# Seven-product units of a fused attention and two-layer MoE kernel: sums in two PSUM tiles by turns, two products of the last unit swapped, no hand-over margin in the planner

## The chip, the cores and the metric

The kernel runs on one core of one Trainium2 chip. The metric is the device time of one execution in microseconds; the kernel before takes 1227.4 us, the median of three runs (1226.18 to 1228.07).

## The reference

An attention block with head mixing before and after the softmax feeds a two-matrix layer with a hard-swish gate, and that feeds a second layer of two up-projections, their product, and two further matrices. All arrays are float32 (B 4, H 12, S 448, D 64).

```python
scores = einsum('bhij,hg->bgij', scale * q @ k.T, w_pre)
attn = softmax(scores)                        # over the last axis
x = einsum('bhij,hg->bgij', attn, w_post) @ v  # then (1792, 768)
h = x @ w_in                                  # 768 -> 2048
g = h * clip(h + 3, 0, 6) / 6
x = g @ w_out                                 # 2048 -> 768
h = (x @ w1) * (x @ w2) @ w3                  # 768 -> 1024 -> 1024
return h @ w_out2                             # 1024 -> 768
```

## The kernel before, in words

Products are made with float32 values split into a high and a low part of a faster format: weight and activation both become a high half (a cast) and a low half (a subtraction), and each product of two values is three matmuls (high by high, high by low, low by high). The kernel multiplies the last two matrices w3 and w_out first (tile `w34`), so the second layer ends with one product by a 1024 x 768 matrix.

The work on the chip goes through these stages: attention, slot by slot (tiles `sc`, `pre`, `post`, `val`); the up-projection by w_in (`up`, for batches 0 and 3 directly, for batches 1 and 2 in seven-product units); the down-projection by w_out (`dn`); `w34`; the second layer's two up-projections in 16 seven-product units (`step`, 8 for each pair of batches, weights in tile `block`); and the final product in 6 seven-product units (3 for each pair of batches, weights in tile `wb`, activations split into `gh` and, in space of the earlier `act` tiles, under that name).

A seven-product unit computes a two by two block product with seven products in place of eight: the function `seven` (L812). Its operands are sums and differences made beforehand on VectorE (`combine` L1096, `rows2` L1257 and the joined weights). Its products are called p1 to p7 in the code, each of K x 3 matmuls of 128 x 448: nine in the units of the `up` and `step` stages (K = 3), twelve in the final stage (K = 4). They add up in three PSUM sums: cs takes p1, p6, p7 and p4 in this order, bs takes p5 and p3, as_ takes p2. In between ScalarE copies the running sum out: k1 after p1, k5 after p5, k6 after p6 (`keep`, the copies of L831). VectorE adds: c11 = as_ + k1 after p2, c12 = bs + k6 after p3, c22 = cs + k5 after p7 (`plus`, L834). p4 adds to cs and must wait for c22; what remains in cs is c21. In the kernel before, cs and bs are the two halves of one PSUM tile `pair`, and as_ is a half of a second tile, `other`, which the unit takes with p2. All PSUM tiles have one shape, [128, 2, 512] float32, and there are four of them. The next unit's p1 may follow as soon as p7 is done.

The order of instructions on every engine is fixed when the program is built, by a planner (`Plan`). Each operation has an engine or a choice of engines, an estimated duration, a priority (a due time) and its predecessors. `Plan.run` (L118) simulates the engines: whenever one is free it takes the waiting operation with the smallest due time that is ready and for whose new buffers there is room. An operation gets ready when its last predecessor has ended plus a hand-over (`HOP`, by the predecessor's engine); if it is for TensorE the hand-over has, unless the predecessor is also on TensorE, a margin of `SLACK` = 400 ns on top. The instructions are then written in the order found, and the engines run them in that order. The semaphores between engines are placed by the language's tile framework from the tiles that instructions read and write.

Due times come from sums of the values in `URGE`: the stage of the up units begins at M1, that of the down products at N1 = M1 + 8 F, `w34` at W0 = N1 + 4 D1, the `step` units at M2 = W0 + W, the final units at N2 = M2 + 16 U2, and offsets such as `gsum` (loads and splits of the final stage's activations), `joined`, `w2` and `wd` (weights) move single kinds of work against these.

Of the kernel before, what the change touches and what calls it, by code (L numbers as in the profile page):

```python
# [20 lines left out]
B, H, S, D = 4, 12, 448, 64  # L21
# [28 lines left out]
def query_order():  # L50
# [9 lines left out]

URGE = dict(pPool=13.287, pACT=19737.186, pDVE=67509.792, pOut=0.285, pGuard=376.043, pCopy=21.334, pRest=107.553, pEvac=52.694, load0=33.466, load=-4.77, gather=-168.494, pre=-140.104, max=-8.516, exp=27.495, norm=15.87, post=2.04, evac=43.38, values=32.185, step=8.267, vload=-54.801, vload0=-30.207, lead=-15.369, begin=-9.6, consts=-75.04, moe=75.017, rows=-53.563, win=-71.545, wout=-22.784, w34=60.311, w2=140.007, unit0=3.845, unit1=6.452, down1=165.725, unit2=13.355, down2=98.964, wo=-88.875, wd=-84.964, narrow=-53.097, sums=98.427, w34us=69.836, pHalf=621.884, halve=10.141, gsum=-54.585, joined=-78.357, pairs=-27.451, lag=-51.378, mix=75.595, wo1=23.777)


SHARED = dict(
# [2 lines left out]
    wo=tuple(f"z{i}" for i in range(9)) + ("w0", "w1", "w2") + tuple(f"y{i}" for i in range(28)),  # L69
# [20 lines left out]
class Plan:  # L90
# [1 line left out]

    HOP = dict(Host=0, PE=200, ACT=150, DVE=130, Pool=130, SP=0)
    DMA_START, DMA_END, FREED = 1100, 910, 180
    SLACK = 400

    def __init__(self, room):
        self.room, self.ops, self.chains = dict(room), [], {}
# [33 lines left out]
    def run(self):  # L132
# [18 lines left out]
        while events:  # L151
            now, done = heapq.heappop(events)
            if done >= 0:
                op = self.ops[done]
                for tag, n in op["gives"].items():
                    self.room[tag] += n
                for x in op["holds"]:
                    x.held -= 1
                    if not x.held:
                        freed.append((now + self.FREED, x.tag))  # L160
                        heapq.heappush(events, (now + self.FREED, -1))
                for n in followers[done]:
                    hop = self.HOP[op["eng"]]
                    if "PE" in n["choice"]:
                        hop = dict(DVE=240 + self.SLACK, ACT=hop + self.SLACK, Pool=hop + self.SLACK, PE=0).get(op["eng"], hop)
                    n["ready"] = max(n["ready"], now + hop)
                    n["left"] -= 1
                    if not n["left"]:
                        for e in n["choice"]:
                            heapq.heappush(waiting[e], (n["prio"], n["id"]))  # L170
                        heapq.heappush(events, (n["ready"], -1))
            if events and events[0][0] <= now:
                continue
            while freed and freed[0][0] <= now:
                tag = freed.popleft()[1]
                for t in PARTS.get(tag, (tag,)):
                    self.room[t] += 1
            for e, heap in waiting.items():
                if free[e] > now:
                    continue  # L180
                skipped = []
                while heap:
                    prio, i = heapq.heappop(heap)
                    op = self.ops[i]
                    if op["eng"]:
                        continue
                    first = next(iter(op["choice"]))
                    homes = None
                    if op["ready"] <= now and (e == first or free[first] > now + URGE["p" + op["wait"]]) and (port <= now or e not in op["port"]) and (not op["apart"] or burst <= now):
                        if op["chain"] is None or self.chains[op["chain"]][0] == i:  # L190
                            homes = self.places(op["new"])
                    if homes is None:
                        skipped.append((prio, i))
                        continue
                    for x, tag in zip(op["new"], homes):
                        x.tag = tag
                        for t in PARTS.get(tag, (tag,)):
                            self.room[t] -= 1
                    if op["chain"] is not None:
                        self.chains[op["chain"]].popleft()  # L200
                        heapq.heappush(events, (now, -1))
                    op["eng"] = e
                    if e == "SP":
                        free[e] = now + op["issue"]
                        wire = max(now + self.DMA_START, wire) + op["choice"][e]
                        end = wire + self.DMA_END
                    else:
                        free[e] = end = now + op["choice"][e]
                        if e in op["port"]:
                            port = end  # L210
                        if op["apart"]:
                            burst = now + op["apart"]
                            heapq.heappush(events, (burst, -1))
                    heapq.heappush(events, (free[e], -1))
                    heapq.heappush(events, (end, i))
                    op["start"] = now
                    order.append(op)
                    break
                for x in skipped:
                    heapq.heappush(heap, x)  # L220
# [10 lines left out]
def attention_moe(ctx: ExitStack, tc, qd, kd, vd, consts, w_in, w_out, w1, w2, w3t, w4, out):  # L231
    nc = tc.nc
# [69 lines left out]
    plan = Plan({**rooms, **{tag: 0 if tag in later else x[3] for tag, x in BUFS.items()}})  # L302
# [506 lines left out]
        def __call__(self):  # L809
            return self.part(self.of.t)  # L810

    def seven(prio, K, ws, xs, before, after=()):  # L812

        pair, other = Buf("up"), Buf("up")
        t, v = Buf("t"), Buf("v")
        cs, bs, as_ = (View(pair, lambda t: t[:, 0, :S]), View(pair, lambda t: t[:, 1, :S]), View(other, lambda t: t[:, 0, :S]))

        def times(n, at, o, start, new=(), after=()):
            (bufs, parts), (xh, xl) = ws[n], xs[n]

            def emit():
                take(*new)
                for c in range(K):
                    wh, wl = (part()[:, col(c)] for part in parts)
                    mm(o(), wh, xh.t[:, c], start and c == 0, False, skip_group_check=not start)
                    mm(o(), wh, xl.t[:, c], False, False, skip_group_check=not start)
                    mm(o(), wl, xh.t[:, c], False, c == K - 1, skip_group_check=not start)
            return plan.add("PE", 607 * K, prio(at), emit, read=(*bufs, xh, xl), new=new, hold=(o.of,), after=after)

        def keep(at, x, k, o, after):  # L830
            return plan.add("ACT", 530, prio(at), lambda: nc.scalar.copy(x.t[:, k], o()), after=after, hold=(pair, x))  # L831

        def plus(at, x, k, o, after):
            return plan.add("DVE", 620, prio(at), lambda: nc.vector.tensor_tensor(out=x.t[:, k], in0=o(), in1=x.t[:, k], op=ALU.add), after=after, hold=(o.of, x))  # L834

        p1 = times(0, 0, cs, True, (pair, t, v), (*before, *after))
        k1 = keep(0, t, 0, cs, (p1,))
        p5 = times(1, 1, bs, True, after=(p1,))
        k5 = keep(1, v, 0, bs, (p5,))
        p6 = times(2, 3, cs, False, after=(k1,))  # L840
        k6 = keep(3, t, 1, cs, (p6,))
        p2 = times(3, 4, as_, True, (other,))
        c11 = plus(4, t, 0, as_, (p2, k1))
        p3 = times(4, 5, bs, False, after=(k5,))
        c12 = plus(5, t, 1, bs, (p3, k6))
        p7 = times(5, 6, cs, False, after=(k6,))
        c22 = plus(6, v, 0, cs, (p7, k5))
        p4 = times(6, 9, cs, False, after=(c22,))
        return t, v, cs, p7, p4, (p2, p3), c11, c12, c22, keep

# [179 lines left out]
    joined = {}  # L1030
# [266 lines left out]
    for pr in range(2):  # L1297
        gs = rows2(pr)
        for m in range(3):
            at = N2 + D2 * (3 * pr + m)  # L1300
            prio = lambda n: at + n * D2 / 10
            t, v, cs, p7, p4, p3, c11, c12, c22, keep = seven(prio, 4, blocks2(at + URGE["wd"], m), gs, before)
            before = (p7,)
            c21 = keep(9, v, 1, cs, (p4,))
            for k, b in enumerate(ORDER[2 * pr:2 * pr + 2]):
                for q, x, y, done in ((0, t, k, (c11, c12)[k]), (1, v, 1 - k, (c21, c22)[k])):
                    plan.add("SP", 900, prio(9), lambda m=m, b=b, q=q, x=x, y=y: nc.sync.dma_start(
                        out=out[col(2 * m + q), b * S:(b + 1) * S], in_=x.t[:, y]), after=(done,), hold=(x,))
# [52 lines left out]
```

## Time and profile before

| | |
|---|---|
| median of three runs | 1227.4 us |
| the profiled execution | 1230.79 us, of which the span from first to last instruction is 1229.0 us |
| granted TensorE clock | 0.999 of full speed over the span |
| TensorE matmul busy | 1185.4 us (96%) |
| TensorE weight load busy | 973.5 us (79%) |
| VectorE, ScalarE, GpSimd busy | 830.4, 630.6, 194.4 us |
| DMA | 259.87 MB, queue of the sync engine 63.2% of 16 engines' span |

PE stands for TensorE's matmuls, PEld for its weight loads, which overlap them, DVE for VectorE, ACT for ScalarE, POOL for GpSimd, SP for the sync engine that issues the transfers. Instructions are grouped by the source line that wrote them, and many come from one helper: all matmuls have line 239, all low halves and differences line 242, casts and plain copies lines 344 (ACT) and 346 (DVE). So tiles tell them apart. "Idle before" is the time the engine had nothing running ahead of an instruction, and the arrow names the engine whose instruction ended that wait.

### The profile page before, as it was taken

To read this page: it belongs to the slowest core of one execution; us is meant where nothing else is said; L and a number is where in the kernel's file an instruction comes from. 1 tells how busy PE (TensorE), PEld (TensorE's weight loads), DVE (VectorE), ACT (ScalarE), POOL (GpSimd) and SP (SyncE) were. 2 spreads that over 40 slices of the span, in tenths; PEclk is the share of its full clock that TensorE was granted. 3 is DMA by queue.
4 is the path that set the end of the run, shared out by engine and by line. 5 is a ranking of instruction groups with operands and counts; after the bars stand their busy time and mean duration, and the time that the engine had idled before them with its cause. 6 is when DMAs were issued, how large, how long until landed. Compare 5 with 4: busy or idle time off the path is not lost. (4 is left out here: it accounts for less than half of the span.)

```text
span 1229.0 us, 29521 instructions
## 1 busy us (share of the span) xinstructions
PE 1185.4 (96%) x11904; PEld 973.5 (79%) x11904; DVE 830.4 (68%) x1364; ACT 630.6 (51%) x1203; POOL 194.4 (16%) x412
## 2 busy tenths in 40 slices
PE   8899999999989999999999999999999999998998
PEld 3556666666658888988999999998889998997887
DVE  3778687776688879743875647676854577478682
ACT  6657666566667566522664344443433354334351
POOL 2474565663231000000000000000000000000000
PEclk9999999999999999999999999999999999999999
DMA  6645653744844566732989798989864438387531
GB/s 217 180 152 198 198 196 133 228 163 157 278 130 156 178 212 218 252 135 76 328 298 326 250 290 307 338 303 346 288 217 149 126 109 305 112 293 244 180 124 68
DMA packets 132945, 259.87 MB, mean 211 GB/s; under 512 B 11880, under 2 KB 75208, under 8 KB 132808
## 3 DMA queue, kind: packets, MB, share of 16 engines
q1 hardware_dynamic: 132808, 257.98, 63.2%
q8 instruction: 94, 1.54, 0.5%
q14 instruction: 43, 0.35, 0.1%
HBM read 151.97 MB, written 67.26 MB: 178 GB/s over the span
## 5 line engine op out<-in xcount | busy, mean ns | idle before, releaser
L239 PE MATMUL up<-act,block 128*128 128x448 f32 x1008 | 208.5, 367 | 3.0 <-ACT t L831 2.4
L239 PEld LDWEIGHTS up<-act,block 128*128 128x128 f32 x1008 | 188.4, 188 | 22.7 <-ACT t L831 4.2
L239 PE MATMUL dn<-gs,act 128*128 128x448 f32 x720 | 151.3, 367 | 0.0
L239 PEld LDWEIGHTS post<-wt,e 60*64 60x64 f32 x5760 | 101.8, 135 | 55.5 <-issue 27.1
L239 PEld LDWEIGHTS dn<-gs,act 128*128 128x128 f32 x720 | 135.2, 188 | 12.2
L239 PE MATMUL up<-act,wide 128*128 128x448 f32 x630 | 135.4, 368 | 1.1 <-DVE v L834 0.3
L502 ACT ACTIVATE e<-pre,m 128x448 f32<-128x448 f32 (+1 forms) x184 | 116.3, 635 | 38.7 <-DVE m L496 18.7
L496 DVE TENSOR_REDUCE m<-pre 128x2 f32<-128x896 f32 (+1 forms) x92 | 99.8, 1085 | 43.1 <-PE pre L239 43.0
L239 PEld LDWEIGHTS up<-act,wide 128*128 128x128 f32 x630 | 117.4, 188 | 14.3 <-issue 1.3
L239 PE MATMUL post<-wt,e 60*64 60x60 f32 x5760 | 108.8, 220 | 10.9 <-issue 3.7
L710 ACT ACTIVATE raw<-raw 128x384 f32<-128x384 f32 (+1 forms) x140 | 72.0, 524 | 77.5 <-DMA raw<-w 38.0
L239 PE MATMUL pre<-g,wih 64*64 64x448 f32 x720 | 95.4, 565 | 6.0 <-issue 1.8
L239 PE MATMUL up<-act,wb 128*128 128x448 f32 x432 | 91.2, 367 | 7.7 <-ACT t L831 3.3
L834 DVE TENSOR_TENSOR t<-up,t 128x448 f32<-128x448 f32 x60 | 37.3, 622 | 90.0 <-PE up L239 85.4
L344 ACT CAST block<-raw 128x384 fp32r<-128x384 f32 x103 | 52.7, 515 | 87.6 <-PE up L239 75.4
L473 POOL MEMSET g<- 4x896 f32 x92 | 76.7, 835 | 117.2 <-PE pre L239 91.2
L239 PEld LDWEIGHTS up<-act,wb 128*128 128x128 f32 x432 | 80.4, 188 | 17.3 <-ACT t L831 5.2
L242 DVE TENSOR_TENSOR block<-raw,block 128x384 fp32r<-128x384 f32 x112 | 60.6, 553 | 28.0 <-ACT block L344 27.9
L718 ACT ACTIVATE raw<-raw 128x768 f32<-128x768 f32 (+1 forms) x70 | 55.7, 795 | 35.0 <-DVE raw L716 34.8
L239 PE MATMUL dn<-gs,wo 128*128 128x448 f32 x336 | 72.9, 368 | 0.0
L722 DVE SCALAR_TENSOR_TENSOR raw<-raw 128x384 int32<-128x384 int32 (+1 forms) x140 | 68.6, 525 | 1.2
L239 PEld LDWEIGHTS dn<-gs,wo 128*128 128x128 f32 x336 | 63.1, 188 | 5.9
(135 smaller groups left out, 1809.4 us busy)
## 6 DMA issues: line engine op xcount, KB each, us to landing
g<-s SPq DMA_DIRECT2D x180, 210.0 KB
raw<-w SPq DMA_DIRECT2D x48, 384.0 KB
graw<-g1dram SPq DMA_DIRECT2D x32, 448.0 KB
raw<-w_out SPq DMA_DIRECT2D x32, 384.0 KB
raw<-w_in SPq DMA_DIRECT2D x28, 384.0 KB
g1dram<-t SPq DMA_DIRECT2D x24, 448.0 KB
raw<-w3t SPq DMA_DIRECT2D x32, 256.0 KB
wraw<-w34dram SPq DMA_DIRECT2D x30, 256.0 KB
```

The lines of the kernel that those rows point to most:

```text
L239: nc.tensor.matmul(o, lhsT=lt, rhs=rh, start=start, stop=stop, **kw)
L242: eng.tensor_tensor(out=o, in0=a, in1=b, op=ALU.subtract)
L344: nc.scalar.copy(o, i)
L473: nc.gpsimd.memset(g.t[:BEFORE], 0.0)
L496: nc.vector.tensor_reduce(out=m.t[used], in_=pre.t[used, :, :S], axis=AX.X, op=ALU.max, negate=True)
L502: nc.scalar.activation(out=e.t[used, a_], in_=pre.t[used, a_, :S], func=ACTF.Exp, bias=m.t[used, a_:a_ + 1], accum_out=z.t[used, a_:a_ + 1])
L710: nc.scalar.mul(value()[:, halves[i]], f(bits(i))[:, :, 1], 2.0 ** -112)
L718: nc.scalar.activation(out=f(y), in_=f(y), func=ACTF.Prelu, alpha=-2.0 ** 32)
L722: two(out=m.t[:, halves[i]], in0=bits(i)[:, :, 0], scalar=29, in1=m.t[:, halves[i]], op0=ALU.logical_shift_right, op1=ALU.bitwise_or)
L834: return plan.add("DVE", 620, prio(at), lambda: nc.vector.tensor_tensor(out=x.t[:, k], in0=o(), in1=x.t[:, k], op=ALU.add), after=after, h ...
```

## The change

Three things. In `seven`, bs moves from the second half of `pair` to the first half of `other`, as_ to the second half of `other`; `other` is now taken with p5 instead of p2, and p2 comes after p5 (before, it had no predecessor in its unit). In the very last unit (`final`) p7 comes before p3, which waits for it. In the planner the margin `SLACK` is gone. Besides, 20 of the values in `URGE` are new.

```diff
-    SLACK = 400
...
-                        hop = dict(DVE=240 + self.SLACK, ACT=hop + self.SLACK, Pool=hop + self.SLACK, PE=0).get(op["eng"], hop)
+                        hop = dict(DVE=240, PE=0).get(op["eng"], hop)
...
-    def seven(prio, K, ws, xs, before, after=()):
+    def seven(prio, K, ws, xs, before, after=(), final=False):
...
-        cs, bs, as_ = (View(pair, lambda t: t[:, 0, :S]), View(pair, lambda t: t[:, 1, :S]), View(other, lambda t: t[:, 0, :S]))
+        cs, bs, as_ = (View(pair, lambda t: t[:, 0, :S]), View(other, lambda t: t[:, 0, :S]), View(other, lambda t: t[:, 1, :S]))
...
-            return plan.add("ACT", 530, prio(at), lambda: nc.scalar.copy(x.t[:, k], o()), after=after, hold=(pair, x))
+            return plan.add("ACT", 530, prio(at), lambda: nc.scalar.copy(x.t[:, k], o()), after=after, hold=(o.of, x))
...
-        p5 = times(1, 1, bs, True, after=(p1,))
+        p5 = times(1, 1, bs, True, (other,), (p1,))
...
-        p2 = times(3, 4, as_, True, (other,))
+        p2 = times(3, 4, as_, True, after=(p5,))
         c11 = plus(4, t, 0, as_, (p2, k1))
-        p3 = times(4, 5, bs, False, after=(k5,))
-        c12 = plus(5, t, 1, bs, (p3, k6))
-        p7 = times(5, 6, cs, False, after=(k6,))
-        c22 = plus(6, v, 0, cs, (p7, k5))
+        p7 = times(5, 5 if final else 6, cs, False, after=(k6,))
+        c22 = plus(5 if final else 6, v, 0, cs, (p7, k5))
+        p3 = times(4, 6 if final else 5, bs, False, after=(k5, p7) if final else (k5,))
+        c12 = plus(6 if final else 5, t, 1, bs, (p3, k6))
...
-            t, v, cs, p7, p4, p3, c11, c12, c22, keep = seven(prio, 4, blocks2(at + URGE["wd"], m), gs, before)
+            t, v, cs, p7, p4, p3, c11, c12, c22, keep = seven(prio, 4, blocks2(at + URGE["wd"], m), gs, before, final=pr == 1 and m == 2)
```

The values of `URGE` that change:

| name | before | after | name | before | after |
|---|---|---|---|---|---|
| pOut | 0.285 | 3.743 | down1 (D1) | 165.725 | 95.531 |
| pCopy | 21.334 | 12.835 | unit2 (U2) | 13.355 | 13.151 |
| pRest | 107.553 | 101.643 | wo | -88.875 | -75.16 |
| moe | 75.017 | 104.397 | narrow | -53.097 | -61.372 |
| win | -71.545 | -87.391 | sums | 98.427 | 107.353 |
| w34 | 60.311 | 71.001 | w34us | 69.836 | 69.981 |
| w2 | 140.007 | 99.201 | gsum | -54.585 | 3.533 |
| unit1 (U1) | 6.452 | 6.717 | joined | -78.357 | 24.31 |
| pairs | -27.451 | -7.78 | lag | -51.378 | -72.907 |
| mix | 75.595 | 92.823 | wo1 | 23.777 | 32.07 |

## Rows read from the trace of the kernel before

**Rows 1.** The page: busy time of the engines, and the slots' row maxima.
```profile
PE 1185.4 (96%) x11904; PEld 973.5 (79%) x11904; DVE 830.4 (68%) x1364; ACT 630.6 (51%) x1203; POOL 194.4 (16%) x412
...
L496 DVE TENSOR_REDUCE m<-pre 128x2 f32<-128x896 f32 (+1 forms) x92 | 99.8, 1085 | 43.1 <-PE pre L239 43.0
```

**Rows 2.** Busy time by stretch: stretch, its length, engines, clock, DMA share, GB/s.
```profile
10.00:345.00 335.00, 319.53 (x7346) 198.86 (x7342) 236.68 (x412) 219.05 (x508) 172.26 (x385) 0.99 0.59 189
...
345.00:600.00 255.00, 246.46 (x1518) 216.78 (x1511) 186.29 (x319) 137.87 (x246) 16.88 (x19) 1.00 0.54 177
600.00:845.00 245.00, 245.00 (x1206) 223.97 (x1205) 157.96 (x277) 114.36 (x180) 1.85 (x1) 1.00 0.90 309
...
1031.00:1111.00 80.00, 78.14 (x382) 71.22 (x381) 51.97 (x89) 31.11 (x57) 0.00 (x0) 1.00 0.67 215
1111.00:1168.00 57.00, 51.93 (x250) 46.27 (x250) 39.32 (x44) 21.59 (x34) 0.00 (x0) 1.00 0.62 202
1168.00:1229.00 61.00, 54.81 (x266) 49.16 (x264) 32.07 (x38) 23.40 (x34) 0.00 (x0) 1.00 0.29 96
```

**Rows 3.** Waits of PE, whole span: us in total, times, longest.
```profile
PE up L239 <- ACT t L831: 9.4, 16, 0.7
...
PE up L239 <- DVE act L242: 2.5, 1, 2.5
PE up L239 <- ACT v L831: 1.9, 3, 0.6
...
PE up L239 <- DVE v L834: 1.7, 2, 1.3
```

**Rows 4.** Timeline of the first `step` unit: start, length, instruction, [idle before].
```profile
901.68 3.81 PE L239 MATMUL up<-act,block 128*128 128x448 f32 x18
...
903.71 0.51 ACT L344 CAST block<-raw 128x384 fp32r<-128x384 f32 x1 [0.47 <-PE up L239]
...
905.53 0.53 ACT L831 COPY t<-up 128x448 f32<-128x448 f32 x1 [1.30 <-PE up L239]
...
906.11 3.88 PE L239 MATMUL up<-act,block 128*128 128x448 f32 x18 [0.62 <-ACT t L831]
```

**Rows 5.** Timeline of PE alone, 840 to 1230 us.
```profile
910.29 104.30 PE L239 MATMUL up<-act,block 128*128 128x448 f32 x504 [0.30 <-ACT t L831]
...
1039.91 2.09 PE L239 MATMUL up<-act,block 128*128 128x448 f32 x9 [0.62 <-ACT t L831]
1042.63 2.08 PE L239 MATMUL up<-act,block 128*128 128x448 f32 x9 [0.62 <-ACT v L831]
1045.33 65.87 PE L239 MATMUL up<-act,block 128*128 128x448 f32 x324 [0.62 <-ACT t L831]
1111.03 0.37 PE L239 MATMUL up<-act,wb 128*128 128x448 f32 x1
...
1116.23 2.02 PE L239 MATMUL up<-act,block 128*128 128x448 f32 x9
1118.09 2.64 PE L239 MATMUL up<-gh,wb 128*128 128x448 f32 x12
```

**Rows 6.** Timeline of all engines, end of the kernel.
```profile
1206.47 14.96 PE L239 MATMUL up<-act,wb 128*128 128x448 f32 x72
...
1221.55 0.62 DVE L834 TENSOR_TENSOR t<-up,t 128x448 f32<-128x448 f32 x1 [4.39 <-PE up L239]
...
1222.76 2.71 PE L239 MATMUL up<-act,wb 128*128 128x448 f32 x12 [1.32 <-DVE v L834]
```

**Rows 7.** Timeline of all engines, entry of the final stage.
```profile
1108.20 3.28 ACT L344 CAST act<-orig 128x1792 fp32r<-128x1792 f32 x2
...
1109.87 3.95 DVE L242 TENSOR_TENSOR act<-orig,act 128x1792 fp32r<-128x1792 f32 x2
```

**Rows 8.** Waits of PE in 0 to 345 us.
```profile
PE post L239 <- issue: 3.7, 5, 2.0
...
PE post L239 <- ACT pth L344: 1.3, 7, 0.2
```

More of the change, by code (lines that the diff above doesn't have):

```diff
@@ L59, in query_order @@
     return order
-URGE = dict(pPool=13.287, pACT=19737.186, pDVE=67509.792, pOut=0.285, pGuard=376.043, pCopy=21.334, pRest=107.553, pEvac=52.694, load0=33.466, load=-4.77, gather=-168.494, pre=-140.104, max=-8.516, exp=27.495, norm=15.87, post=2.04, evac=43.38, values=32.185, step=8.267, vload=-54.801, vload0=-30.207, lead=-15.369, begin=-9.6, consts=-75.04, moe=75.017, rows=-53.563, win=-71.545, wout=-22.784, w34=60.311, w2=140.007, unit0=3.845, unit1=6.452, down1=165.725, unit2=13.355, down2=98.964, wo=-88.875, wd=-84.964, narrow=-53.097, sums=98.427, w34us=69.836, pHalf=621.884, halve=10.141, gsum=-54.585, joined=-78.357, pairs=-27.451, lag=-51.378, mix=75.595, wo1=23.777)
+URGE = dict(pPool=13.287, pACT=19737.186, pDVE=67509.792, pOut=3.743, pGuard=376.043, pCopy=12.835, pRest=101.643, pEvac=52.694, load0=33.466, load=-4.77, gather=-168.494, pre=-140.104, max=-8.516, exp=27.495, norm=15.87, post=2.04, evac=43.38, values=32.185, step=8.267, vload=-54.801, vload0=-30.207, lead=-15.369, begin=-9.6, consts=-75.04, moe=104.397, rows=-53.563, win=-87.391, wout=-22.784, w34=71.001, w2=99.201, unit0=3.845, unit1=6.717, down1=95.531, unit2=13.151, down2=98.964, wo=-75.16, wd=-84.964, narrow=-61.372, sums=107.353, w34us=69.981, pHalf=621.884, halve=10.141, gsum=3.533, joined=24.31, pairs=-7.78, lag=-72.907, mix=92.823, wo1=32.07)
 SHARED = dict(
```

## The prediction

> **What bounds the kernel now.** I read the page's engine lines first. TensorE (PE) is busy 1185.4 of 1229.0 us, 96%, so there are 43.6 us in which it does nothing, and an edit that leaves every matmul in place can win back only part of them [rows 1]. Then the stretches, to see where those 43.6 us lie. In 10 to 345 us (attention) PE misses 335 - 319.5 = 15.5 us; in 345 to 600 (first seven-product units) 8.5; in 600 to 845 (down projection) nothing, with the DMA at 0.90; in the last three stretches, 1031 to the end, 80 + 57 + 61 less 78.1 + 51.9 + 54.8 = 13.1 [rows 2]. (Sums over windows count a matmul on an edge in full, so they are good to some tenths.) The granted clock is 1.00 of full speed, so the 2.4 GHz level, in all of these, and the clock is no term here.
>
> Then what PE waits for in the unit stages. Nineteen waits, 9.4 + 1.9 = 11.3 us, end on a ScalarE (ACT) copy of line 831, so on k1, k5 or k6; one of 2.5 us ends on a VectorE (DVE) low half of `act`, and of two on a DVE addition of line 834 the longer is 1.3 [rows 3].
>
> Why do those copies come late? The timeline of the first unit shows it. PE runs 18 matmuls from 901.68 to 905.49 without a break: p1 and p5, nine each, at 1.86 us a product (504 matmuls in 104.30 us [rows 5]). So p1 ends near 903.6. The copy k1 needs p1 alone, ACT's cast before it ended at 904.22, and yet k1 starts at 905.53, as p5 ends, after 1.30 us of idleness that ended on PE [rows 4]. p5 writes the other half of the same PSUM tile. The wait goes by tile: a reader of one half waits for the last product issued before it that writes either half. PE then stands 0.62 us until p6 at 906.11.
>
> **The change part by part.** My sum is made against the profiled execution, 1230.8 us (span 1229.0 and 1.8 around it), and is carried over as a difference to the median, 1227.4, which lies 3.4 below it.
>
> *Two tiles by turns.* cs stays in `pair`, bs moves to `other`, where as_ is. p1, p5, p6, p2 now alternate between the tiles, so k1 runs under p5, k5 under p6 and k6 under p2 (a copy takes 0.53 us, a product of nine matmuls 1.86, one of twelve 14.96 / 6 = 2.49 [rows 4 to 6]). A wait of 0.62 costs more than 0.62: at 1039.91, 1042.63 and 1045.33 products follow each other by 2.72 and 2.70 us where an undisturbed one takes 1.86, so 0.85 each [rows 5]. Fifteen of the 19 are of this form and length, 9.3 of the 11.3 us; the rows show four of them [rows 4, 5]. That is 15 x 0.85 = 12.7 us gained. The other four share 2.0 us (the first, 0.30, stands at 910.29 [rows 5]); they are no 0.62, so another ACT instruction had a part in them, and I take half, 1.0, between 0 and 2.0.
>
> What does the new grouping make wait? c11 reads `other`, and p3 now writes `other`, mostly right behind p2, so c11 will start at p3's end, one product late. In its place c12 loses such a wait: today it waits for p7, as the end of the kernel shows, where c12 starts at 1221.55 as p7's last matmul ends, although p3 ended a product earlier [rows 6]. Behind c11 on DVE stand c12, c22 and the low halves of weights; c22 waits for p7 anyway, one product after p3, so p4 is not later. The low halves today stand behind c12 just as long. I take 0 (bounds: 0 and one wait of 0.85 in each of 30 units, 25.5, which today's equal stall of c12, hidden almost everywhere, makes unlikely). `other` is also taken at p5 instead of p2 and kept until c12: with four PSUM tiles two units fit whole, so 0; where direct products share the tiles (the eight units of 345 to 600) a full house would cost at most a wait each, 6.8.
>
> *p2 behind p5.* p2 now depends on p5; before it could run ahead of its unit. That is a loss. At the entry of the final stage PE runs p2 of the new unit (`act,wb`, 1111.03 to 1116.2, with the 2.5 us stall inside), then p4 of the old unit (`block`, 1116.23), and only at 1118.09 p1 (`gh,wb`) [rows 3, 5]. Without it PE has nothing until p4: one slot of 2.5 us goes from cover to the path. The three waits in a row at 1039 to 1045 say the same of that unit: nothing was left to put between p6, p3 and p7, so its p2 had gone ahead; there I take 1.0 of its 1.86. Tile names do not separate units elsewhere, so I allow one more case at half a slot, 1.2. Loss 4.7 us, bounds 0 and one slot of 2.49 at each of the five places where new operands begin, 12.4.
>
> *Final unit, p7 before p3.* Today p7 is the last of 72 matmuls, c12 and c22 follow on DVE from 1221.55, and p4 starts at 1222.76, after 1.32 us [rows 6]. With p7 first, c22 (0.62 us) runs under p3 (2.49), and p4 follows p3 at once. As above a wait costs 0.23 more than its length: gain 1.5, bounds 1.3 and 1.7. The stores behind it keep their length.
>
> *No margin (SLACK).* It moves no work, but lets the planner place an instruction 0.4 us sooner behind its input. In the units it hardly matters, products being 1.86 us. In attention, where PE waits are many and short (3.7 us in five, 1.3 in seven [rows 8]), order may get tighter or brittle. Those 15.5 us bound the gain; the loss is bounded by one more wait of the commonest kind, 1.3 / 7 = 0.19, in each of the 92 slots [rows 1, 8], 17.1. PE is 95% busy on both sides of it; I take 0.
>
> *Due times.* The down stage gets D1 95.5 for 165.7, so weight side work falls elsewhere in it; PE has no idleness there to win, and DMA at 0.90 could only lose. The operand splits of the final stage (`gsum`) fall due 58 later. They are dear: a low half of `act` 3.95 / 2 = 1.98 us of DVE, a cast 3.28 / 2 = 1.64 of ACT [rows 7]; a difference is the same DVE instruction over as many elements, so I price it alike. I take 0 between the present 2.5 us stall going away and the rival below.
>
> Sum: -12.7 - 1.0 - 1.5 + 4.7 = -10.5 us: 1220.3 for a profiled execution like this one, 1216.9 against the median, say 1217.
>
> **Where a page and a row differ.** The copy that starts at p5's end says that the guard goes by tile [rows 4]. The Trainium skill (PSUM — Partial Sum Buffer, section "PSUM bank collisions raise a hardware error") says to guard PSUM by bank and quadrant, other banks being free; its table of specifications gives 512 FP32 values to a bank, which makes the two halves of this tile two banks. By that rule k1 would never have waited for p5 and regrouping would change nothing, the first rival; by the row it gains 12.7 us.
>
> **The rivals.** (A change inside 0.2%, 2.5 us, is what a measurement of this kernel can hardly tell from none: faster is under 1224.9, slower over 1229.9.)
>
> *Regrouping does nothing*, because the copies wait for order on ACT and not for the tile: only the end (-1.5) and the lost cover of p2 (+4.7) remain, 1227.4 + 3.2 = 1230.6. Against it stand the 1.30 us in which ACT had nothing else to do before k1, ended by PE [rows 4]. Chance 0.05.
>
> *Late splits at the two entries of the final stage*, the slower side. Seven low halves and four differences are 11 x 1.98 = 22 us of DVE for each pair of batches, a unit gives 7 x 2.49 = 17.4 us of PE. Started only when due, they leave PE waiting 22 - 17.4 plus a first cast and low half (3.6), 8.2 us per entry; two entries 16.4, 13.9 more than now: 1230.8. It turns the sign once the two entries wait more than 10.5 + 2.5 = 13.0 us together. For it: `gsum` alone moves by 58, and the entry already stalls on just this. Against: DVE has 28 us of idleness in 1031 to 1111 to work ahead [rows 2]. Chance 0.13.
>
> *Attention without the margin gets brittle*: the 17.1 us above, 1234.0. Against: of the present 15.5 us [rows 2], no releaser has more than the 3.7 us [rows 8]. Chance 0.10.
>
> *More than forecast*: half of attention's 15.5 us goes, and the 2.5 us stall: 1216.9 - 7.7 - 2.5 = 1206.7. Chance 0.20.
>
> **How the numbers follow.** The forecast holds 0.52, with 1211 to 1223 as its own range (the bounds of p2's cover and of the small waits). Faster by over 0.2% are nearly all of it (0.50), the better case (0.20) and the milder half of the late splits or brittle attention (0.04): 0.74. Slower are the rest of those two and part of the first rival, 0.15; within 0.2%, 0.11. The range, 1206 to 1231, takes in the better case and the full price of late splits, and leaves out brittle attention and the outer ends.
>
> **What would show it.** Right: the waits of PE on line 831 fall from 19 to at most five; in the first unit k1 starts within 0.2 us of p1's end unless a cast holds ACT; c11 starts where p3 ends, c12 right behind it; the last matmuls run without a break before p4; at the entries of the second half and of the final stage PE shows new waits on DVE additions. Wrong: the 0.62 us waits still stand, or PE's idle time in 10 to 345 or 1100 to 1190 us has grown by more than the 11 us that the rest gives.

## The result and the profile after

The changed kernel takes 1208.4 us (median of four runs, 1207.2 to 1211.9) against 1226.8 us for the kernel before (1225.2 to 1228.1): a ratio of 0.9859, 95% interval 0.9838 to 0.9880. It is 18 us faster where the prediction said 10.5.

The page of the kernel after, engine line, as in [rows 1]:

```profile
PE 1175.1 (97%) x11904; PEld 975.3 (81%) x11904; DVE 826.0 (68%) x1372; ACT 625.6 (52%) x1196; POOL 198.0 (16%) x411
```

Its stretches, with the columns of [rows 2]:

```profile
10.00:345.00 335.00, 322.41 (x7511) 200.95 (x7507) 241.05 (x429) 225.31 (x521) 175.21 (x388) 1.00 0.60 192
345.00:600.00 255.00, 251.17 (x1413) 227.03 (x1414) 199.59 (x344) 148.10 (x255) 19.45 (x16) 0.99 0.61 206
...
1031.00:1111.00 80.00, 75.88 (x367) 69.79 (x366) 55.13 (x81) 32.07 (x53) 0.00 (x0) 0.98 0.69 224
1111.00:1168.00 57.00, 56.38 (x276) 51.39 (x275) 43.33 (x49) 26.00 (x39) 0.00 (x0) 1.00 0.59 181
```

PE's missing time falls from 15.5 to 12.6 us in 10 to 345 us and from 8.5 to 3.8 in 345 to 600. Its largest group of waits in the unit stages over the whole span (us, times, longest), to hold against [rows 3]:

```profile
PE up L238 <- DVE v L833: 5.5, 3, 4.1
```

No wait of PE ends on a copy any more; there were 19, 11.3 us. (The line numbers are one lower, since SLACK's line is gone: copies 830, additions 833.) The waits on additions have grown from 1.7 to 5.5 us. The timeline of all engines shows the first `step` unit, the entry of the final stage and the last unit:

```profile
889.15 0.51 ACT L343 CAST block<-raw 128x384 fp32r<-128x384 f32 x1 [0.47 <-PE up L238]
...
889.57 0.53 ACT L830 COPY t<-up 128x448 f32<-128x448 f32 x1
...
892.77 0.54 ACT L830 COPY t<-up 128x448 f32<-128x448 f32 x1 [0.23 <-PE up L238]
...
896.43 0.62 DVE L833 TENSOR_TENSOR t<-up,t 128x448 f32<-128x448 f32 x1 [2.70 <-PE up L238]
...
897.44 0.62 DVE L833 TENSOR_TENSOR t<-up,t 128x448 f32<-128x448 f32 x1
...
1091.38 2.02 DVE L241 TENSOR_TENSOR act<-orig,act 128x1792 fp32r<-128x1792 f32 x1
1093.32 0.69 DVE L241 TENSOR_TENSOR wb<-wraw,wb 128x512 fp32r<-128x512 f32 x1
1093.92 0.62 DVE L833 TENSOR_TENSOR v<-up,v 128x448 f32<-128x448 f32 x1
...
1197.41 0.62 DVE L833 TENSOR_TENSOR v<-up,v 128x448 f32<-128x448 f32 x1 [1.79 <-PE up L238]
```

k1 (889.57) starts behind a cast on ACT, no longer behind p5; c11 (896.43) starts only after p3, c12 (897.44) soon behind it. At the entry c22 (1093.92) stands on DVE behind a low half of `act` and one of a weight. In the last unit c22 (1197.41) runs under p3. The timeline of PE alone, to hold against [rows 5]:

```profile
887.12 125.65 PE L238 MATMUL up<-act,block 128*128 128x448 f32 x621
1013.71 76.76 PE L238 MATMUL up<-act,block 128*128 128x448 f32 x378 [0.94 <-DVE v L833]
1094.59 3.59 PE L238 MATMUL up<-act,block 128*128 128x448 f32 x9 [4.12 <-DVE v L833]
...
1184.88 17.43 PE L238 MATMUL up<-act,wb 128*128 128x448 f32 x84
```

The first 621 matmuls of `step` run without a break, where the kernel before stopped for copies at 906.11 and 910.29 [rows 4, 5]; the last 84 run through, p4 included. The 0.94 and 4.12 us waits are p4's, on c22. The second stands at the entry of the final stage. The first comes after 621 = 69 x 9 matmuls, ten units less their last p4; with eight units for each pair of batches it is the second unit of the second pair, not the one where new operands begin.

The two profiled spans differ by 23.2 us, 4.8 more than the medians: the profiled run of the kernel before, 1230.8 us, is slower than the four that gave its median. PE's busy time is 10.3 of the 23.2 (1185.4 less 1175.1, with as many matmuls), its idle time 12.9. Where they lie follows from when a stage's first or last matmul starts: 6.7 us are won by attention's last `post` (363.7, now 357.0 us), 7.7 more by the first `dn` (598.1, now 583.7), 0.2 to the first matmul of the `step` units (901.7, now 887.1), 5.5 to the first `gh` of the final stage (1118.1, now 1098.0) and 3.1 to the end of PE's work. The forecast had nothing in the first of these.

### The profile page after: what moved, and what is told of

It is laid out like the page before. It is cut to its first block, busy times and chain, and to the rows that moved or that the text cites. A ratio compares the mean times of both kernels' runs of the same rounds, so it can differ in the third digit from the quotient of the medians.

```text
span 1205.8 us, 29514 instructions
## 1 busy us (share of the span) xinstructions
PE 1175.1 (97%) x11904; PEld 975.3 (81%) x11904; DVE 826.0 (68%) x1372; ACT 625.6 (52%) x1196; POOL 198.0 (16%) x411
## 4 chain that ended last, share of the span: by engine, by line
PE 82%; DMA 7%; DVE 3%; ACT 3%; issue 2%; POOL 2%; SPq 2%; POOLq 0%; ACTq 0%; DVEq 0%
PE up L238 40%; PE dn L238 20%; PE w L238 6%; PE post L238 5%; PE sc L238 4%; PE val L238 4%; PE pre L238 4%; DMA g<-s 2%; DMA first<-w_in 1%; SPq L481 1%; DMA xdram<-x 1%; ACT e L501 1%; DMA qraw<-qd 1%; ACT ptl L343 1%; DMA kraw<-kd 1%
## 5 line engine op out<-in xcount | busy, mean ns | idle before, releaser
L238 PE MATMUL up<-act,block 128*128 128x448 f32 x1008 | 206.0, 366 | 5.1 <-DVE v L833 5.1
L238 PE MATMUL dn<-gs,act 128*128 128x448 f32 x720 | 147.9, 367 | 0.0
L238 PE MATMUL up<-act,wide 128*128 128x448 f32 x630 | 142.8, 368 | 2.0 <-POOL act L241 1.6
L238 PEld LDWEIGHTS up<-act,wide 128*128 128x128 f32 x630 | 117.9, 188 | 13.7 <-POOL act L241 2.1
```

What stands on the lines that cost most here:

```text
L238: nc.tensor.matmul(o, lhsT=lt, rhs=rh, start=start, stop=stop, **kw)
```

## The experiments

The change has four parts: the grouping of the sums (with the dependency of p2), the swap in the final unit, the margin, and the due times. All kernels compute the whole reference; only order and placing differ. The kernel before had medians of 1228.6, 1224.6 and 1225.5 us beside the three sets of runs. "Post" and "dn" are the starts of attention's last `post` and of the first `dn` matmul in the profiled run, as above.

| kernel | grouping | swap | margin off | new due times | median us | ratio (95%) | post | dn |
|---|---|---|---|---|---|---|---|---|
| before | | | | | 1226.8 | 1 | 363.7 | 598.1 |
| layout_only | x | | | | 1223.5 | 0.9957 (0.9941 to 0.9974) | 362.8 | 592.1 |
| layout_final | x | x | | | 1223.3 | 0.9994 (0.9976 to 1.0012) | 361.7 | 591.1 |
| margin_only | | | x | | 1238.9 | 1.0079 (1.0053 to 1.0104) | 359.7 | 604.7 |
| dues_only | | | | x | 1240.5 | 1.0094 (1.0072 to 1.0116) | 360.6 | 612.7 |
| all_but_layout | | | x | x | 1240.8 | 1.0097 (1.0076 to 1.0118) | 357.6 | 603.4 |
| all_but_dues | x | x | x | | 1227.3 | 1.0023 (1.0007 to 1.0040) | 360.5 | 598.1 |
| all_but_margin | x | x | | x | 1216.0 | 0.9931 (0.9905 to 0.9956) | 363.8 | 595.9 |
| all_but_final | x | | x | x | 1208.8 | 0.9884 (0.9854 to 0.9914) | 354.1 | 580.6 |
| after | x | x | x | x | 1208.4 | 0.9859 (0.9838 to 0.9880) | 357.0 | 583.7 |

### The grouping by itself

The kernel before with the new `seven`, without the swap; margin and due times as before. Its core, the views written short:

```diff
-        cs, bs, as_ = (pair 0, pair 1, other 0)
+        cs, bs, as_ = (pair 0, other 0, other 1)
-        p2 = times(3, 4, as_, True, (other,))
+        p2 = times(3, 4, as_, True, after=(p5,))
```

> The kernel before with only the new grouping of the sums (bs and as_ in one PSUM tile, cs in the other, p2 behind p5); order of p3 and p7, margin and due times as before. Theory (waits go by tile): the 19 waits of PE on copies of line 831 fall to five or fewer, the start of the down products comes 5 to 7 us sooner, and the time falls by 9.0 us (12.7 + 1.0 gained, 4.7 lost by p2) to about 1218; the end keeps its 1.3 us wait. Rival (copies wait only for their turn on ACT): the 19 waits stay and the time is 1226 to 1231. Rival (most of the 18 us came from due times): under 3 us gained.

Measured 0.9957, about 5 us faster. Its waits of PE and PE's timeline (this kernel keeps SLACK's line, so copies are line 831):

```profile
PE up L239 <- DVE v L834: 8.1, 4, 4.6
...
PE up L239 <- ACT v L831: 0.2, 1, 0.2
```

```profile
1028.04 78.23 PE L239 MATMUL up<-act,block 128*128 128x448 f32 x378 [2.33 <-DVE v L834]
1110.86 3.73 PE L239 MATMUL up<-act,block 128*128 128x448 f32 x9 [4.59 <-DVE v L834]
1114.39 3.41 PE L239 MATMUL up<-gh,wb 128*128 128x448 f32 x12
```

The copy waits go from 19 to one, and the first `dn` starts 6.0 us sooner. In the same two places as in the full change p4 now waits for c22, 2.33 and 4.59 us. Both halves of the theory hold, the gain and the price; the price is larger than expected.

> The kernel before with the new grouping and the swap of the last unit, old margin and due times. Grouping alone took 5.1 us. Theory: the swap takes another 0.9 to 1.5 us at the very end and nothing elsewhere, 1222.4. Rival: no difference to the grouping alone (1223.5).

With the swap as well 0.9994. The two ratios stand against different runs of the kernel before; the medians themselves agree (1223.5 and 1223.3). Grouping and swap together are therefore worth between nothing and 5 us, not the 10.5 forecast.

### Margin and due times by themselves

```diff
-                        hop = dict(DVE=240 + self.SLACK, ACT=hop + self.SLACK, ...
+                        hop = dict(DVE=240, PE=0).get(op["eng"], hop)
```

> The kernel before with only the planner's margin of 0.4 us taken out. Theory (the margin cost attention time): the last matmul of attention, at 380.1 us before and 368.8 after the whole change, comes 5 to 11 us sooner, the 19 waits on copies stay or grow, and the time falls by 4 to 9 us. Rival (due times gave the attention gain): attention ends within 2 us of before, time within 3 us of it. Rival (brittle order, as the prediction priced it): slower by up to 17.

Measured 1.0079: attention's last matmul ends at 374.9 us instead of 380.1, and then PE stands. The timeline of PE, and that of all engines (here ACT) just before:

```profile
381.42 9.83 PE L238 MATMUL up<-act,wide 128*128 128x448 f32 x31 [3.88 <-ACT act L343]
395.46 1.12 PE L238 MATMUL up<-act,wide 128*128 128x448 f32 x2 [4.21 <-DVE act L241]
```

```profile
376.46 0.56 ACT L709 ACTIVATE raw<-raw 128x384 f32<-128x384 f32 x1 [0.30 <-DMA raw<-w_in]
...
378.72 0.55 ACT L709 ACTIVATE raw<-raw 128x384 f32<-128x384 f32 x1 [1.70 <-DMA raw<-w_in]
...
379.80 0.54 ACT L709 ACTIVATE raw<-raw 128x384 f32<-128x384 f32 x1 [0.54 <-DMA raw<-w_out]
380.25 0.83 ACT L717 ACTIVATE raw<-raw 128x768 f32<-128x768 f32 x1
380.98 0.67 ACT L343 CAST act<-stg 128x240 fp32r<-128x240 f32 x2
```

The casts of `act` that PE waits for stand on ACT's queue behind operations on weights that wait for their DMA. Attention is over sooner; the operands of the first units are not ready sooner (these two casts start at 380.98 us here, at 380.4 and 380.8 in the kernel before). The clock falls too: it is 0.70 of full speed over 380 to 400 us, where the kernel before has 1.00.

> The kernel before with only the 20 new values of URGE. Theory (due times give nothing by themselves): within 3 us of before, attention's end within 3 us, waits on copies as many as before. Rival (due times gave the attention gain): attention ends 7 to 11 us sooner and the time falls by about 8. Rival of late splits: PE waits 5 to 16 us at the entries of the final stage, slower.

The new due times alone: 1.0094, with 22 copy waits and one of 5.5 us on a cast of `act`. Both together, with the old grouping:

> The changed kernel with the old grouping of the sums and the old order of p3 and p7 in the last unit, so margin and due times alone. If parts add up: 18.4 less the 10.5 of layout and swap, so 8 us gained, about 1219, with the waits on copies back at 15 or more. If the margin was what kept the old grouping's waits hidden, more of them than 19 and no gain. If due times were made for the new grouping alone, slower than before.

Measured 1.0097. Attention gains 6.1 us (post 357.6), nearly as much as in the full change, and all of it is gone by the first `dn`, which starts 5.3 us later than before. PE's waits in 345 to 604 us of this kernel:

```profile
PE up L238 <- ACT t L830: 5.7, 9, 0.7
PE up L238 <- ACT v L830: 3.8, 5, 1.2
PE up L238 <- POOL act L241: 1.6, 3, 0.8
PE up L238 <- ACT act L343: 1.4, 1, 1.4
```

Fourteen copy waits, 9.5 us, where the kernel before has seven, 4.3 us, in the same stage. The rest of the 11.4 us lost there is in part the waits on `act` and in part the clock (0.91 over 380 to 400 us); how it divides was not settled.

### Each part taken out of the full change

> The changed kernel with the 20 old due times: new grouping, swapped last products, no margin. The margin alone took 5.2 us off attention's end and then lost 14 us in waits between attention and the down products, 8.1 of it on splits of act at 381 and 395 us. Theory (the waits on copies drove the loss): with the new grouping these waits go too, attention ends at 370 to 376 us, PE waits under 4 us before the down products, time 1212 to 1218. Rival (due times of the old order are what makes those splits late): the two waits of about 4 us on act stay, no wait on copies, time 1222 to 1230.

With the old due times 1.0023: one copy wait is left (0.3 us), but at 383.84 PE waits 5.49 us and at 396.36 3.44 us, the same two places as in margin_only (the profile puts the first down to a VectorE operation on weights, the second to a low half of `act`).

> The changed kernel with the margin of 0.4 us put back. Theory (the margin is worth attention's 7 us and nothing in the units): attention ends near 378 to 381 us, the waits on copies stay at zero, time 1214 to 1218. Rival (due times were chosen for an order without margin): waits on act and pool splits at 382 to 392 us as with the due times alone, time 1222 to 1232.

With the margin back 0.9931. Attention's last `post` and last matmul fall back to 363.8 and 380.5 us, those of the kernel before. So the margin's absence is worth 1208.4 against 1216.0, some 8 us, once the rest is in place, and by itself it costs 10. (The ten runs with the margin spread from 1211.7 to 1225.3 us.)

> The changed kernel with p3 before p7 in the last unit too. Theory: the order before the last unit is the same, and p4 waits for c22 again: p7 last, c22 0.62 us behind it, so 0.8 to 1.0 us of idleness and a restart, 1.1 us more in the profile's last part; the old 1.32 us do not come back whole because c12 no longer waits for p7. Rival (swap worth nothing): the last matmul ends as before within 0.3 us of the changed kernel's.

Without the swap 0.9884; 1208.8 against 1208.4, not to be told apart by medians. In the profile the stretch from the first `gh` to PE's end is 105.3 instead of 104.3 us, and p4 waits 0.72 us. PE's timeline:

```profile
884.00 128.35 PE L238 MATMUL up<-act,block 128*128 128x448 f32 x621
1013.28 78.22 PE L238 MATMUL up<-act,block 128*128 128x448 f32 x378 [0.93 <-DVE v L833]
...
1201.24 2.71 PE L238 MATMUL up<-act,wb 128*128 128x448 f32 x12 [0.72 <-DVE v L833]
```

Up to the last unit this kernel's engines run the same instructions in the same order as the full change, and still its last `post` is 2.9 us earlier. Differences of some 3 us between single profiles are thus no evidence on the program.

### Which due times

Old values of moe, win, pairs, lag, mix, wo1 and unit1 (the first units) in the full change, then old values of down1, unit2, w34, w34us, w2, wo, narrow, sums, gsum and joined (the later ones); pOut, pCopy and pRest stay new in both:

> The changed kernel with the old values of the seven due times of the first up stage (moe, win, pairs, lag, mix, wo1, unit1), the other 13 new. Theory (the up stage's due times are what keeps the splits of act in time when the margin is gone): waits of 3 to 6 us on act or raw weights come back between 378 and 397 us, 8 to 15 us lost, 1216 to 1224. Rival (the late due times matter): within 3 us of 1208.

> The changed kernel with the old values of the ten due times of the down, w34, step and final stages (down1, unit2, w34, w34us, w2, wo, narrow, sums, gsum, joined). Theory: the up stage is as in the changed kernel (down products begin at 580 to 585 us), the waits on c22 at the two entries go from 5.1 to 8 us as with the margin alone taken out, so 3 to 4 us lost, 1211. Rival (gsum's later due time, which the prediction feared, helps or costs more): over 6 us either way.

The first loses all (1.0032, 1.0015 to 1.0049; 1228.6 us), the second 7 us (0.9926, 0.9897 to 0.9954; 1215.6). With the old times of the first units PE's timeline has the two waits again:

```profile
374.42 2.74 PE L238 MATMUL up<-act,wide 128*128 128x448 f32 x12
382.61 0.74 PE L238 MATMUL up<-act,wide 128*128 128x448 f32 x1 [5.45 <-ACT act L343]
...
395.05 1.11 PE L238 MATMUL up<-act,wide 128*128 128x448 f32 x2 [3.53 <-DVE act L241]
```

The cast that ends the first wait, from the timeline of all engines, with old times and in the full change:

```profile
382.16 0.79 ACT L343 CAST act<-stg 128x240 fp32r<-128x240 f32 x2 [0.44 <-DMA stg<-xdram]
```

```profile
379.73 0.82 ACT L343 CAST act<-stg 128x240 fp32r<-128x240 f32 x2 [1.47 <-DMA stg<-xdram]
```

It waits for attention's last output to come back from DRAM: the write is issued at 375.12 us and the read at 380.00 with old times, at 375.49 and 377.64 in the full change. So the new times bring this cast forward by 2.4 us. They also move other work: PE's timeline in the full change, whose attention ends at 368.8 us, has three groups of nine matmuls on `half`, 6.1 us in all, between attention and that cast:

```profile
368.72 2.08 PE L238 MATMUL up<-half,wide 128*128 128x448 f32 x9
...
371.24 2.02 PE L238 MATMUL up<-half,mixed 128*128 128x448 f32 x9
...
375.61 2.02 PE L238 MATMUL up<-half,mixed 128*128 128x448 f32 x9
```

With the old times three such groups run before attention's last matmul, at 356.50, 367.30 and 370.86; behind it are the twelve at 374.42 and then the wait. How much each of the two effects is worth was not separated. The clock adds to the loss: 0.68 over 380 to 400 us with old times, 1.00 in the full change, 6.4 us by these two numbers.

With the old later times the first `dn` is where it is in the full change (584.8 us), and the waits on additions are 8.6 us in four instead of 5.5 in three. So the new later times as a whole, the later `gsum` among them, did not hurt the entry; the rival of late splits said the opposite of `gsum`. Which of the ten helps was not separated.

### Where as_ lies, and p2 ahead again

A test of the rule by which the waits go: as_ in the second half of `pair`, beside cs, and p2 bound to p1 only (views written short).

```diff
-        cs, bs, as_ = (pair 0, other 0, other 1)
+        cs, bs, as_ = (pair 0, other 0, pair 1)
-        p2 = times(3, 4, as_, True, after=(p5,))
+        p2 = times(3, 4, as_, True, after=(p1,))
```

> The changed kernel with as_ in the second half of cs's tile (and p2 behind p1) in place of bs's tile. Theory (a reader waits for the last product issued before it that writes either half of its tile): k6 now starts at p2's end, not at p6's, c11 no longer waits for p3; k6 is hidden under p3 except in the last unit, where p7 follows p2 and PE waits about 0.6 us; the other waits stay, time within 4 us of the changed kernel's 1208. Rival (copies and additions wait for their own product or their turn only): k6 and c11 start as in the changed kernel.

Ratio 0.9969 (0.9946 to 0.9992), 1221.1 us; the places were right, the time was expected within 4 us of 1208. In the profiles 2.6 us are lost by attention's last `post` (359.6), 8.4 by the first `step` matmul (895.5) and 14.5 by the end of PE's work; why is open. The timeline of all engines in one `step` unit, and the end of PE's own:

```profile
955.13 0.53 ACT L830 COPY t<-up 128x448 f32<-128x448 f32 x1 [1.30 <-PE up L238]
...
955.70 0.62 DVE L833 TENSOR_TENSOR t<-up,t 128x448 f32<-128x448 f32 x1 [1.28 <-ACT t L830]
```

```profile
1183.68 12.60 PE L238 MATMUL up<-act,wb 128*128 128x448 f32 x60 [1.64 <-ACT t L830]
...
1209.23 7.55 PE L238 MATMUL up<-act,wb 128*128 128x448 f32 x36 [0.62 <-ACT t L830]
```

p6 ended near 953.1, p2 at 954.9; k6, which reads p6's sum, started at 955.13 after 1.30 us of idleness that ended on PE. In the full change k6 runs under p2. The addition at 955.70, c11, starts right behind k6 while p3 still runs; in the full change it starts at p3's end. One move of a sum to the other half, with p2 bound to p1, brings the 1.30 us back at another copy, and PE's 0.62 us with it.

Last, p2 put ahead of p5 again in three units, the first with new operands in the second half of `step` and the first of each pair in the final stage. In the kernel before p2 had no predecessor and p5 followed p1; here p5 follows p2 as well:

```diff
+        p2 = times(3, 4, as_, True, (other,)) if early else None
+        p5 = times(1, 1, bs, True, () if early else (other,), (p1, p2) if early else (p1,))
```

> The changed kernel with p2 free to go ahead in the three units where new operands begin late in the kernel (first step unit of the second pair, first final unit of each pair): there p2 takes the tile and p5 comes after p2. Theory (what the prediction priced as lost cover of p2): the waits of 0.94 us at 1013.7 and 4.12 at 1094.6 on c22 shrink to under 2 us together, no wait on a copy comes back, 2 to 4.5 us gained, about 1205. Rival (c22 is late by DVE's queue and p2's operands are no earlier): a wait on a low half of act in their place, no gain.

Ratio 0.9980 (0.9958 to 1.0001); the runs reach from 1215.4, the profiled one, to 1227.9, so this comparison settles little on the time. The waits it was to remove still stand in PE's timeline:

```profile
987.70 24.03 PE L238 MATMUL up<-act,block 128*128 128x448 f32 x116 [0.82 <-DVE act L241]
1014.59 76.74 PE L238 MATMUL up<-act,block 128*128 128x448 f32 x378 [2.85 <-DVE v L833]
1095.45 3.56 PE L238 MATMUL up<-act,block 128*128 128x448 f32 x9 [4.12 <-DVE v L833]
...
1153.33 11.85 PE L238 MATMUL up<-act,wb 128*128 128x448 f32 x49 [2.92 <-DVE v L833]
1168.22 4.87 PE L238 MATMUL up<-act,wb 128*128 128x448 f32 x23 [3.04 <-DVE act L241]
```

Ahead of 987.70 the `step` stage has 505 = 56 x 9 + 1 matmuls: p2 of the ninth unit, now second in its unit, stops after its first matmul for its own low half. The wait at 1014.59 (0.94 us in the full change) is at the end of the tenth unit and could not be reached this way, since p2 of the eleventh was not freed. At the entry of the final stage p2 did not get ahead of the old unit's p4, and the 4.12 us stay; the low halves that its operands need stand on DVE around c22, so that they were probably no earlier than c22 itself. At the third place two waits of 2.92 and 3.04 us stand where the full change has one of 0.49. So the rival, that p2's operands are no earlier, holds in part: waits on low halves of `act`, 3.9 us in two, come on top. Whether p2 bound to nothing, with p5 free as in the kernel before, would cover the 4.12 us was not run.

## Why the prediction was right, and where it was not

**Two tiles by turns: the mechanism is right.** Copy waits are 19 to 24 in every kernel with the old grouping and none to three in every one with the new, whatever margin and due times do. as_with_cs shows directly that a copy waits for the last product issued before it into either half of its tile. The waits removed are 11.1 us long in layout_only; 13.7 were priced, with 0.23 us more for each. The 1.30 us in [rows 4] and the 1.30 us of k6 in as_with_cs show that this kernel's guards go by the tile. The Trainium skill (PSUM — Partial Sum Buffer, section "PSUM bank collisions raise a hardware error") would have PSUM guarded a bank at a time; guards set so would leave out both waits, and what the kernel would take with them no run shows.

**c11 and c12 at nothing: right.** c11 starts after p3, c12 1.01 us later, and no wait of PE on either follows.

**p2 behind p5: right at one entry, and too small a price by itself.** Without the wait in the last unit (1.3 us before, 0.7 in layout_only, none after) the waits on additions grew from 0.4 to 7.4 us in layout_only while the 2.5 us wait on the split went away, so 4.5 us net. The long wait also lowers the clock (last section), which the prediction had called no term: the nine matmuls after it took 3.73 us instead of 2.02 and the next twelve 3.41 instead of 2.64 [rows 5], 2.5 us more. That is 7.0 where 4.7 was priced. In the full change it is 5.5 - 0.4 - 2.5 = 2.6 us and 3.59 - 2.02 = 1.6 of clock, 4.2. By these waits and this clock layout_only should win 11.1 + 0.6 - 7.0 = 4.7 us, and it won 5.1 by medians; the 0.23 us for each restart are not seen on top. What is late in the full change is c22 on DVE, behind a split; that p2 ahead of p4 would cover it is not shown, since in entry_p2 p2 got ahead of p4 at neither place. The new waits were foretold on VectorE additions at the entries of the second half and of the final stage: the second is there, the first stands at the end of the unit after the entry, where the kernel before has p2 of a later unit as cover.

**The final swap: 1.0 for 1.5 in the profiles, and not seen in the medians.** The old wait of 1.32 [rows 6] had two parts. The grouping alone takes c12 off p7, which leaves 0.72; the swap removes those 0.72 us and the 0.2 to 0.3 that a restart costs.

**Margin and due times at nothing: the step that failed.** The prediction priced "no margin" at 0 between -15.5 and +17.1 and the due times at 0, each as if it stood alone. Alone they cost 10 and 12 us. Put on top of grouping and swap together, they turn 1223.3 into 1208.4 us: 15 of the 18. Of these the due times win 7 without the other (1216.0), the margin's absence without the other loses 4 (1227.3). Without the margin attention's last `post` comes 3 to 7 us sooner than in the kernel before. With the new times of the first units PE has other products to run until the casts of `act` are there, and the first of those casts comes 2.4 us sooner (without them, 3.5 and 5.5 us of waiting and a lower clock behind it). The new grouping keeps the products from stopping at copies (without it, 14 such waits in that stage). Without any one of the three, 8 to 32 us are lost by the medians, 9 to 29 by the ratios. So the grouping, which the forecast gave all the gain, by itself brings no more than 5 us, and some 30 (1240.8 against 1208.4) as the condition of the rest. That the measured time is within 9 us of the forecast is in part luck: this omission and the overpriced net gain of the grouping have opposite signs.

**The rivals.** "Regrouping does nothing" fell. "Late splits" fell: the wait at the entry of the final stage is 4.1 us, not 8.2, and it is 4.9 with the ten later due times old. "Attention brittle without the margin" is real in margin_only and all_but_dues, but just behind attention, in the first units, and the due times avert it. "More than forecast" (1206.7) gives the time nearly, by half of its mechanism at most: attention's last `post` comes 6.7 us sooner, but of PE's missing 15.5 us in 10 to 345 only 2.9 went. The 2.5 us stall gave way to one of 4.1.

**What stays open.** Why dues_only, with the margin, waits 5.5 us on a cast of `act` where all_but_layout, without it, waits 1.4; how the loss of the old grouping in the first units divides; and how much of the 3 us by which profiles of the same order differ stands in any one stage's figure above.

## What to carry to other kernels

When a copy starts exactly at the end of a product whose sum it does not read, look at what shares its tile, and alternate tiles between neighbours in the stream; then look at what the new grouping makes the additions and the next unit wait for. A scheduler's margin and its due times are not neutral edits to be priced one by one: ask which operand the earlier consumer will wait for, on which in-order queue or transfer, and whether another part of the change puts that operand forward or gives the consumer other work until then. A change of several parts needs the kernels with one part left out, not only those with one part alone: here no single part showed more than 5 us of the 18.

## What the hardware did that was not expected

**A long wait costs more than its length.** In 1094 to 1098 us of the kernel after, behind the 4.12 us wait, the granted clock is 0.60; behind the 5.45 us wait of old_up_dues it is 0.50, the 1.2 GHz level; behind the 2.5 us wait of the kernel before it stays 1.00 (1115 to 1119 us). The length alone does not decide: in margin_only the wait in the same place is 2.49 us, the clock behind it 0.60 (1122 to 1126 us), and the eleven matmuls take 3.84 us instead of 2.51. Stretches of PE in the kernel after, columns: stretch, length, PE, clock, DMA share, GB/s:

```profile
1090.00:1094.00 4.00, 0.47 (x3) 1.00 0.45 146
1094.00:1098.00 4.00, 3.41 (x10) 0.60 0.25 76
1098.00:1102.00 4.00, 4.00 (x21) 0.98 0.37 114
```

The Trainium skill (TensorE: Matmul & The Clock Gate, section "HAM oscillation — how this bites in real kernels") warns that idle gaps send TensorE back to its lower clock; these rows agree. The prediction should have priced it in its rival of late splits. Runs of one kernel differ with it as well: entry_p2 took 1215.4 us at a mean clock of 0.997 and 1227.9 at 0.990.

**The same matmuls at two spacings.** With the clock at 1.00, the same operands and the same instruction order, the first 621 `block` matmuls took 125.65 us in the kernel after (202.3 ns each) and 128.35 in all_but_final (206.7). The next 378 took 76.76 and 78.22. The kernel before has both: 207 ns in the 504 from 910.29 (104.30 us) and 203 in the 324 from 1045.33 (65.87 us [rows 5]). One weight load takes 187 to 188 ns at either spacing, so it is not that. Between the two kernels with the same order it makes 2.7 + 1.5 = 4.2 us; of the 5.5 that the `step` stage won against the kernel before it is about 2.9, the 4.6 ns in each of the first 621. Since all_but_final has the whole change but the swap and runs at 207, the grouping, the margin and the due times do not set it. Its cause is open.
